# Decode attention with a gating MLP on one core: extra rows of w4 on five engines, values 512-wide on four column groups, y as one wide row

## The chip, the core and the metric

The kernel runs on one core of a Trainium2 chip. The metric is the device time of one execution in microseconds, from the first to the last instruction on that core as the harness takes it; a profile of one execution shows where it goes. In what follows PE is TensorE (the matrix engine), DVE is VectorE, ACT is ScalarE, POOL is GpSimd and SP is SyncE, which issues the loads. PSUM is the memory that matmuls write to.

## The reference

One token attends to the last 4096 positions of a cache of 32 heads, and the result is multiplied by a gate that a small MLP computes from the same token:

```python
x  = A_x                                  # 1 x 1 x 512, bf16
xn = layernorm(x)
q  = xn @ wq                              # 32 heads of 128
p  = softmax(q . k[last 4096] * 128**-0.5)
o  = p @ v[last 4096]                     # 32 heads of 128
s  = o.reshape(4096) @ wo                 # 4096 -> 512
h  = gelu(layernorm(xn) @ w1)             # S = 1: every one of its four shifted quarters becomes zero
x1 = xn + shifted(h) @ w2                 # the shifted h is zero
g  = silu(x1 + gelu(layernorm(x1) @ w3) @ w4)   # w3: 512 x 1376, w4: 1376 x 512
out = x + s * g
```

With one position the shifts leave only zeros, so the kernel never reads w1. Keys and values are 64 MB of the 78.84 MB that the kernel reads; wq and wo are 4 MB each, and the MLP's weights the rest.

## The kernel before

The heads are worked in eight groups of four (G = 4). In stage s the keys of group s are loaded and scored while the values of group s - 2 are used (LAG = 2). A tile of keys or values is 128 partitions by CP = 128 positions by 128 elements: 4 MB. All the large loads go out on SP's queue in program order; K tiles have three buffers, V tiles two.

The weights come first. The 1376 rows of w4 are ten blocks of 128 and 96 rows, and wq is read in two blocks of rows:

```python
w4_sb = wts.tile([P, 11, D], BF16, name="w4_sb")
load(w4_sb[:, 0:10, :], B_w4[0:10 * P, :].rearrange("(p c) n -> p c n", p=P))
load(w4_sb[0:96, 10, :], B_w4[10 * P:F, :])
...
load(wq_sb[:].rearrange("p c n -> p (c n)"), A_wq.rearrange("(a b c) n -> b a (c n)", a=2, c=KC))
```

The scores of a group are shared: VectorE multiplies and sums 64 to 80 of the 128 positions (`k_vector`, in four parts), and TensorE transposes the others, ScalarE copies them out of PSUM, and TensorE multiplies them with q (`k_turn`, `k_scores`). The values are multiplied in one of two forms. Groups 0 and 2 (`MOVED`) take the 16 columns of probabilities as the stationary operand and stream 512 elements of V; all 32 of these matmuls add into the same 16 rows of PSUM, and `v_add` then picks four 128-wide pieces out. The others take V as the stationary operand, in 128 narrow matmuls:

```python
def v_part(g, v, c0=0, c1=CP):
    s = st[g]
    if g in MOVED:
        s["ov"] = ps_o.tile([4 * G, 4, Dh], FP32, tag="oT", name="ov")
        for c in range(0, CP, 4):
            nc.tensor.matmul(s["ov"][:], lhsT=s["pT"][:, c:c + 4, :].rearrange("p i a -> p (i a)"),
                             rhs=v[:, c:c + 4, :], start=(c == 0), stop=(c == CP - 4))
        s["ov_sb"] = sm_pool.tile([4 * G, 4, Dh], FP32, tag="ov_sb", bufs=1, name="ov_sb")
        nc.scalar.copy(out=s["ov_sb"][:], in_=s["ov"][:])
        return
    if c0 == 0:
        s["oT"] = ps_o.tile([P, G], FP32, tag="oT", name="oT")
    for c in range(c0, c1):
        nc.tensor.matmul(s["oT"][:], lhsT=v[:, c, :], rhs=s["pT"][:, c, :], start=(c == 0),
                         stop=(c == CP - 1))
```

The output row y = o @ wo is added up in blocks of heads. Heads 0-15 are a wide row (16 matmuls of 1 x 512) in stage 6; heads 16-23 are 128-wide matmuls on four column groups (`y_block`). 320 rows of wo from head 24 on come by two loads over five DMA engines (`load_few`); the rest of wo comes as single rows of heads (`load_rows`):

```python
blocks = [(0, 16), (16, 8), (24, 8)]
...
def load_few():
    t = wo_blk[few_block]
    for c in range(2):
        r0 = few_h * P + c * FEW // 2
        load(t[32 * c:32 * c + 4 * NE],
             A_wo[r0:r0 + FEW // 2, :].rearrange("(b a t) n -> a b (t n)", b=4, a=NE))
```

The stages, with the parts of keys and softmax cut:

```python
if s < NG:
    k_open(s); k_vector(s, kn, 0); keys(0, 2)
    if s > 1:
        sm_den(s - 2); sm_rden(s - 2)
    if h - 1 in MOVED:                 # h = s - 2
        v_add(h - 1); v_out(h - 1)
    keys(2, 4); k_vector(s, kn, 1); ...
    keys(4, nb); k_scores(s, nb - 1); sm_own(s)
    if s > 0:
        sm_exp(s - 1)
    k_vector(s, kn, 2); ...; k_vector(s, kn, 3)
    if h >= 0:
        v_part(h, v)
    sm_max(s)
    if s == 6:
        y_wide(0, 0, 16)
    if h >= 0 and h not in MOVED:
        v_out(h)
elif s == NG:
    sm_den(NG - 2); sm_rden(NG - 2); sm_turn(NG - 1)
    ox_spread(1); sm_exp(NG - 1); ox_pick(1)
    y_block(1)
    rows_add(y_ps, one_f, y_row, False)
    v_part(h, v); v_out(h)
    ox_spread(few_block); sm_den(NG - 1); sm_rden(NG - 1)
    ox_pick(few_block); ox_few(few_block)
else:
    v_part(h, v, 0, cuts[1])           # cuts = (0, 64, 112, 128)
    y_block(few_block)
    for r in range(h_part, H - G):
        y_head(r)
    for c0, c1 in zip(cuts[1:], cuts[2:]):
        v_part(h, v, c0, c1)
    v_out(h)
    for r in range(H - G, H):
        y_head(r)
```

PE, DVE and ACT run these instructions in this order (`manual_schedule`).

Of the kernel before, what the change touches and what calls it, by code (L numbers as in the profile page):

```python
# [25 lines left out]
MOVED = (0, 2)  # L26
# [3 lines left out]
def kernel(  # L30
# [28 lines left out]
    assert F == 10 * P + 96  # L59
# [30 lines left out]
    w4_sb = wts.tile([P, 11, D], BF16, name="w4_sb")  # L90
    load(w4_sb[:, 0:10, :], B_w4[0:10 * P, :].rearrange("(p c) n -> p c n", p=P))
    load(w4_sb[0:96, 10, :], B_w4[10 * P:F, :])
    wq_sb = wts.tile([P, KC, HD], BF16, name="wq_sb")

    load(wq_sb[:].rearrange("p c n -> p (c n)"), A_wq.rearrange("(a b c) n -> b a (c n)", a=2, c=KC))
# [80 lines left out]

    x_f = small.tile([P, KC], FP32, name="x_f")
# [8 lines left out]
    perm = wts.tile([P, P // 2, 2], BF16, name="perm")  # L186
    nc.vector.tensor_copy(out=perm[:], in_=ident_bf[:].rearrange("k (a b) -> k b a", a=2))
# [24 lines left out]
    chunks = [(P, slice(r, 10 * P, 10)) for r in range(10)]  # L212
    chunks += [(96, slice(10 * P, F, 1))]
    a_ps = ps_misc.tile([P, 11], FP32, tag="misc", name="a_ps")
    for j, (m, cols) in enumerate(chunks):
        for c in range(KC):
            nc.tensor.matmul(a_ps[0:m, j:j + 1], lhsT=w3_sb[:, c, cols], rhs=z3_bf[:, c:c + 1],  # L217
                             start=(c == 0), stop=(c == KC - 1))
    a_bf = small.tile([P, 11], BF16, name="a_bf")
    nc.scalar.activation(out=a_bf[:, 0:10], in_=a_ps[:, 0:10], func=ACT.Gelu_apprx_tanh)  # L220
    nc.scalar.activation(out=a_bf[0:96, 10:11], in_=a_ps[0:96, 10:11], func=ACT.Gelu_apprx_tanh)
# [5 lines left out]
    for i, (m, _) in enumerate(chunks):  # L227
        nc.tensor.matmul(hr_ps[:], lhsT=a_bf[0:m, i:i + 1], rhs=w4_sb[0:m, i, :], start=False,  # L228
                         stop=(i == len(chunks) - 1))
# [31 lines left out]

    few = const.tile([P, 2, 32], BF16, name="few")
    nc.vector.memset(few[:], 0.0)
    for c in range(2):
        nc.vector.tensor_copy(
            out=few[:, c, 0:4 * NE].rearrange("p (a b) -> p a b", b=4),
            in_=ident_bf[:, 4 * NE * c:4 * NE * (c + 1)].rearrange("p (b a) -> p a b", b=4))


# [18 lines left out]
                            op0=ALU.add, op1=ALU.mult)  # L290

# [93 lines left out]
    blocks = [(0, 16), (16, 8), (24, 8)]  # L385
    few_block = 2
    few_h = blocks[few_block][0]
    FEW = 8 * 8 * NE
    h_part = few_h + FEW // P

    r_part = FEW % P
# [6 lines left out]
    def load_few():  # L398
        t = wo_blk[few_block]
        for c in range(2):  # L400
            r0 = few_h * P + c * FEW // 2
            load(t[32 * c:32 * c + 4 * NE],
                 A_wo[r0:r0 + FEW // 2, :].rearrange("(b a t) n -> a b (t n)", b=4, a=NE))

# [3 lines left out]
    def load_rows(h, n):  # L408
        if h == h_part:
            load(wo_rows[r_part:P, 0, :], A_wo[h * P + r_part:(h + 1) * P, :])  # L410
            h, n = h + 1, n - 1
        load(wo_rows[:, h - h_part:h - h_part + n, :],
             A_wo[h * P:(h + n) * P, :].rearrange("(h p) n -> p h n", p=P))
# [3 lines left out]
    def v_part(g, v, c0=0, c1=CP):  # L417
        s = st[g]
        if g in MOVED:
            s["ov"] = ps_o.tile([4 * G, 4, Dh], FP32, tag="oT", name="ov")  # L420
            for c in range(0, CP, 4):
                nc.tensor.matmul(s["ov"][:], lhsT=s["pT"][:, c:c + 4, :].rearrange("p i a -> p (i a)"),  # L422
                                 rhs=v[:, c:c + 4, :], start=(c == 0), stop=(c == CP - 4))
            s["ov_sb"] = sm_pool.tile([4 * G, 4, Dh], FP32, tag="ov_sb", bufs=1, name="ov_sb")
            nc.scalar.copy(out=s["ov_sb"][:], in_=s["ov"][:])  # L425
            return
        if c0 == 0:
            s["oT"] = ps_o.tile([P, G], FP32, tag="oT", name="oT")
        for c in range(c0, c1):
            nc.tensor.matmul(s["oT"][:], lhsT=v[:, c, :], rhs=s["pT"][:, c, :], start=(c == 0),  # L430
                             stop=(c == CP - 1))

    def v_add(g):
        s = st[g]
        s["oT"] = ps_misc.tile([P, G], FP32, tag="misc", name="oT")
        for j in range(4):
            nc.tensor.matmul(s["oT"][:], lhsT=s["ov_sb"][:, j, :], rhs=ident_f[0:4 * G, G * j:G * j + G],  # L437
                             start=(j == 0), stop=(j == 3))

    def v_out(g):  # L440
        h = G * g
        b = [i for i, (h0, _) in enumerate(blocks) if h >= h0][-1]
        if b not in o_blk:
            o_blk[b] = sm_pool.tile([P, blocks[b][1]], BF16, tag=f"o{b}", bufs=1, name="o")
            if b == few_block:
                nc.gpsimd.memset(o_blk[b][:], 0.0)
        c = h - blocks[b][0]
        if g >= NG - 2:
            nc.vector.tensor_tensor(out=o_blk[b][:, c:c + G], in0=st[g]["oT"][:], in1=st[g]["rden"][:],  # L449
                                    op=ALU.mult)  # L450
            return
        for k in range(G):
            nc.scalar.mul(o_blk[b][:, c + k:c + k + 1], st[g]["oT"][:, k:k + 1], st[g]["rden"][:, k:k + 1])  # L453
# [24 lines left out]
    def ox_few(i):  # L478
        of_ps = ps_misc.tile([64, 8], FP32, tag="misc", name="of_ps")
        nc.tensor.matmul(of_ps[:], lhsT=few[:].rearrange("p a b -> p (a b)"), rhs=ox_blk[i][:],  # L480
                         start=True, stop=True)
        of = sm_pool.tile([64, 8], BF16, tag="of", bufs=1, name="of")
        nc.vector.tensor_copy(out=of[:], in_=of_ps[:])
        ox_blk[i] = of


# [4 lines left out]
    def y_wide(i, t0, t1):  # L491
        n = blocks[i][1]
        if t0 == 0:
            yr[i] = ps_tr.tile([1, D], FP32, tag="pt", name="yr_ps")
        for t in range(t0, t1):
            nc.tensor.matmul(yr[i][:], lhsT=ox_blk[i][:, t:t + 1], rhs=wo_blk[i][:, t, :], start=(t == 0),  # L496
                             stop=(t == n - 1))
        if t1 == n:
            nc.scalar.copy(out=y_row[:], in_=yr[i][:])

    def y_block(i):
        for t in range(8):
            rows_add(y_ps, ox_blk[i][:, t:t + 1], wo_blk[i][:, t, :], False)

    def y_head(h):
        rows_add(y_ps, o_blk[few_block][:, h - few_h:h - few_h + 1], wo_row(h), h == H - 1)
# [7 lines left out]
    for s in range(NG + LAG):  # L514
# [3 lines left out]
        if s == LAG:  # L518
            wts_guard.__exit__(None, None, None)
            v_pool = ctx.enter_context(tc.tile_pool(name="v", bufs=V_BUFS))  # L520
            wo_blk[few_block] = v_pool.tile([64, 8, D], BF16, tag="wo_few", bufs=1, name="wo_few")
            nc.gpsimd.memset(wo_blk[few_block][:], 0.0)
            wo_rows = v_pool.tile([P, H - h_part, D], BF16, tag="wo_rows", bufs=1, name="wo_rows")
            nc.gpsimd.memset(wo_rows[0:r_part, 0, :], 0.0)
        if last:
            load_rows(h_part, 2)
            v = load_kv(v_pool, A_v_cache, h, cuts)
            for r, n in ((H - G, 2), (H - 2, 1), (H - 1, 1)):
                load_rows(r, n)
        elif h >= 0:  # L530
            v = load_kv(v_pool, A_v_cache, h)
# [4 lines left out]
        if h == 5:  # L536
            load_wo(1)
            load_few()

        if s < NG:  # L540
# [14 lines left out]
            if h - 1 in MOVED:  # L555
                v_add(h - 1)
                v_out(h - 1)
# [18 lines left out]
            if s == 6:  # L576
                y_wide(0, 0, 16)
            if h >= 0 and h not in MOVED:
                v_out(h)
        elif s == NG:  # L580

            sm_den(NG - 2)
            sm_rden(NG - 2)
            sm_turn(NG - 1)
            ox_spread(1)
            sm_exp(NG - 1)
            ox_pick(1)
            y_block(1)
            rows_add(y_ps, one_f, y_row, False)
            v_part(h, v)  # L590
            v_out(h)
            ox_spread(few_block)
            sm_den(NG - 1)
            sm_rden(NG - 1)
            ox_pick(few_block)
            ox_few(few_block)
        else:
            v_part(h, v, 0, cuts[1])
            y_block(few_block)
            for r in range(h_part, H - G):  # L600
                y_head(r)
            for c0, c1 in zip(cuts[1:], cuts[2:]):
                v_part(h, v, c0, c1)
            v_out(h)
            for r in range(H - G, H):
                y_head(r)
# [36 lines left out]
```

## Time and profile before

| what | value |
|---|---|
| time, median of 3 runs | 194.84 us (194.61 to 195.24) |
| span of the profiled execution | 193.2 us |
| busy PE, DVE, ACT, POOL | 132.6, 143.8, 87.1, 6.4 us |
| read from HBM | 78.84 MB, 408 GB/s over the span |
| DMA packets | 4725, of them 1466 under 2 KB |
| mean granted clock of PE | 0.702 |

The profile is one execution on this core. Its page gives the busy time of each engine, then the span in 40 slices of 4.83 us with a digit for the busy tenths, then the DMA queues, then the groups of instructions by line: busy us and mean ns of one, then the idle time before them and what ended it. A timeline line gives start, length, engine, source line, and output<-inputs. "issue" is a wait that the profile doesn't explain. The granted clock is TensorE's own, as a share of full speed. Matmuls overlap, so the mean duration of one is longer than what it costs in a row.

### The profile page before, as it was taken

To read this page: it belongs to the slowest core of one execution; us is meant where nothing else is said; L and a number is where in the kernel's file an instruction comes from. 1 tells how busy PE (TensorE), PEld (TensorE's weight loads), DVE (VectorE), ACT (ScalarE), POOL (GpSimd) and SP (SyncE) were. 2 spreads that over 40 slices of the span, in tenths; PEclk is the share of its full clock that TensorE was granted. 3 is DMA by queue.
4 is the path that set the end of the run, shared out by engine and by line. 5 is a ranking of instruction groups with operands and counts; after the bars stand their busy time and mean duration, and the time that the engine had idled before them with its cause. 6 is when DMAs were issued, how large, how long until landed. Compare 5 with 4: busy or idle time off the path is not lost.

```text
span 193.2 us, 4769 instructions
## 1 busy us (share of the span) xinstructions
PE 132.6 (69%) x2123; PEld 102.3 (53%) x2123; DVE 143.8 (74%) x162; ACT 87.1 (45%) x195; POOL 6.4 (3%) x14
## 2 busy tenths in 40 slices
PE   0549763977736579798898938840878879845792
PEld 0444463866625433486884428740768257733771
DVE  0560208999999999999999999990899999931201
ACT  2003002888896360468568044731574077813000
POOL 2110008000000000000000000000000000000000
PEclk9999955588755557978559995855576696755555
DMA  6999999999999999999999999999999999999980
GB/s 205 417 472 427 397 427 453 421 427 424 434 431 434 434 433 421 434 427 434 424 431 434 431 434 407 461 431 434 431 427 426 427 424 407 458 417 377 416 326 8
DMA packets 4725, 79.13 MB, mean 410 GB/s; under 512 B 666, under 2 KB 1466, under 8 KB 1722
## 3 DMA queue, kind: packets, MB, share of 16 engines
q1 hardware_dynamic: 4554, 78.84, 96.0%
q8 instruction: 16, 0.26, 0.5%
q10 hardware_dynamic: 152, 0.00, 0.0%
q14 instruction: 3, 0.02, 0.0%
HBM read 78.84 MB, written 0.00 MB: 408 GB/s over the span
## 4 chain that ended last, share of the span: by engine, by line
DVE 50%; DMA 24%; PE 16%; issue 5%; ACT 3%; POOL 1%; SPq 0%; ACTq 0%; POOLq 0%
DVE S L310 29%; DVE prod L308 16%; DMA kv<-in_A_k_cache_dram 14%; DMA kv<-in_A_v_cache_dram 8%; PE oT L430 3%; PE yr_ps L496 3%; ACT kt L326 2%; DMA x_bf<-in_A_x_dram 2%; PE qT_ps L244 2%; PE hr_ps L228 2%; PE a_ps L217 1%; PE pt L324 1%; PE hr_ps L225 1%; PE sT L332 1%; DVE S L346 1%
## 5 line engine op out<-in xcount | busy, mean ns | idle before, releaser
L310 DVE TENSOR_REDUCE S<-prod 128x20 f32<-128x2560 bf16 (+2 forms) x32 | 82.2, 2570 | 1.1
L326 ACT COPY kt<-pt 128x1024 bf16<-128x1024 bf16 (+1 forms) x56 | 54.5, 1007 | 20.9 <-PE pt L324 20.3
L324 PE MATMUL pt<-ident_bf,kv 128*128 128x128 bf16 x444 | 47.1, 276 | 7.1 <-DMA kv<-in_A_k_cache_dram 7.1
L308 DVE TENSOR_TENSOR prod<-kv,q_bc 128x2560 bf16<-128x2560 bf16 (+2 forms) x32 | 43.5, 1360 | 7.6 <-DMA kv<-in_A_k_cache_dram 4.9
L324 PEld LDWEIGHTS <-kv 128*128 128x128 bf16 x444 | 38.0, 127 | 9.2 <-DMA kv<-in_A_k_cache_dram 7.9
L332 PE MATMUL sT<-qT_bf,kt 128*128 128x4 bf16 x444 | 20.6, 168 | 16.9 <-ACT kt L326 16.3
L332 PEld LDWEIGHTS <-kt 128*128 128x128 bf16 x444 | 17.1, 103 | 24.5 <-ACT kt L326 24.1
L430 PE MATMUL oT<-pT,kv 128*128 128x4 bf16 x768 | 21.8, 166 | 7.6 <-issue 5.5
L430 PEld LDWEIGHTS <-kv 128*128 128x128 bf16 x768 | 21.1, 103 | 9.6 <-issue 5.7
L422 PE MATMUL ov<-kv,pT 128*16 128x512 bf16 x64 | 16.6, 425 | 0.0
L370 ACT ACTIVATE pT<-S,mb 128x128 bf16<-128x128 f32 x32 | 13.9, 570 | 0.3
L453 ACT ACTIVATE o<-oT,rden 128x1 bf16<-128x1 f32 x24 | 4.3, 261 | 15.5 <-PE oT L430 9.0
L422 PEld LDWEIGHTS <-pT 128*16 128x16 bf16 x64 | 6.1, 98 | 9.5 <-issue 3.5
L449 DVE TENSOR_TENSOR o<-oT,rden 128x4 bf16<-128x4 f32 x2 | 0.3, 162 | 12.4 <-PE oT L430 12.4
L341 ACT ACTIVATE own<-sT,par 128x48 f32<-128x48 f32 (+2 forms) x32 | 7.6, 361 | 3.6 <-PE sT L332 3.1
L370 ACT ACTIVATION_READ_ACCUMULATOR pT<-S,mb 128x1 f32 x32 | 8.2, 255 | 0.0
L231 DVE COPY hr<-hr_ps 1x512 f32<-1x512 f32 x1 | 0.7, 679 | 8.3 <-PE hr_ps L228 8.3
L425 ACT COPY ov_sb<-ov 16x512 f32<-16x512 f32 x2 | 1.1, 575 | 12.1 <-PE ov L422 12.1
L437 PE MATMUL oT<-ident_f,ov_sb 16*128 16x4 f32 x16 | 2.9, 301 | 4.1 <-DVE rden L381 4.1
L496 PE MATMUL yr_ps<-wo,ox 128*1 128x512 bf16 x16 | 4.9, 476 | 1.2 <-DVE ox L474 1.2
L220 ACT ACTIVATE a_bf<-a_ps 128x10 bf16<-128x10 f32 x1 | 0.2, 179 | 12.1 <-PE a_ps L217 12.1
L354 PE MATMUL mt_ps<-ident_f,m 128*1 128x128 f32 x8 | 2.8, 354 | 3.3 <-DVE rden L381 3.3
(117 smaller groups left out, 92.0 us busy)
## 6 DMA issues: line engine op xcount, KB each, us to landing
kv<-in_A_k_cache_dram SPq DMA_DIRECT2D x7, 4096.0 KB, 29.4
kv<-in_A_v_cache_dram SPq DMA_DIRECT2D x7, 4096.0 KB, 33.8
wq_sb<-in_A_wq_dram SPq DMA_DIRECT2D x1, 4096.0 KB, 18.4
kv<-in_A_k_cache_dram SPq DMA_DIRECT2D x2, 2048.0 KB, 22.6
wo<-in_A_wo_dram SPq DMA_DIRECT2D x1, 2048.0 KB
kv<-in_A_v_cache_dram SPq DMA_DIRECT2D x1, 2048.0 KB, 11.9
kv<-in_A_v_cache_dram SPq DMA_DIRECT2D x1, 1536.0 KB, 15.0
w_sb<-in_B_w_dram SPq DMA_DIRECT2D x1, 1376.0 KB
```

Source lines behind the costliest of these rows:

```text
L228: nc.tensor.matmul(hr_ps[:], lhsT=a_bf[0:m, i:i + 1], rhs=w4_sb[0:m, i, :], start=False, stop=(i == len(chunks) - 1))
L308: nc.vector.tensor_tensor(out=prod[:, 0:m, :], in0=kn[:, rows, :], in1=q_bc[:, g:g + 1, :].to_broadcast([P, m, Dh]), op=ALU.mult)
L310: nc.vector.tensor_reduce(out=st[g]["S"][:, rows], in_=prod[:, 0:m, :], axis=AX.X, op=ALU.add)
L324: nc.tensor.transpose(pt[:, c - c0, :], kn[:, c, :], ident_bf[:])
L326: nc.scalar.copy(out=kts[b][:, 0:c1 - c0, :], in_=pt[:, 0:c1 - c0, :])
L332: nc.tensor.matmul(st[g]["sT"][:, c - nd(g), :], lhsT=kt[:, c - c0, :], rhs=qT_bf[:, G * g:G * g + G], start=True, stop=True)
L341: nc.scalar.mul(s["own"][:, 0:m, a], s["sT"][:, 0:m, a], par[:, a:a + 1])
L370: nc.scalar.activation(out=s["pT"][:, :, a], in_=s["S"][:], func=ACT.Exp, scale=scale, bias=mb[:, a:a + 1], accum_out=s["sum"][:, a:a + 1])
L422: nc.tensor.matmul(s["ov"][:], lhsT=s["pT"][:, c:c + 4, :].rearrange("p i a -> p (i a)"), rhs=v[:, c:c + 4, :], start=(c == 0), stop=(c == ...
L430: nc.tensor.matmul(s["oT"][:], lhsT=v[:, c, :], rhs=s["pT"][:, c, :], start=(c == 0), stop=(c == CP - 1))
L453: nc.scalar.mul(o_blk[b][:, c + k:c + k + 1], st[g]["oT"][:, k:k + 1], st[g]["rden"][:, k:k + 1])
L496: nc.tensor.matmul(yr[i][:], lhsT=ox_blk[i][:, t:t + 1], rhs=wo_blk[i][:, t, :], start=(t == 0), stop=(t == n - 1))
```

## The change

It moves where the uneven load of five DMA engines falls, and puts values and y into forms with fewer and wider matmuls. TensorE's program goes from 4,120 rows to 3,026.

- 320 rows of w4 are loaded over five engines, as 320 rows of wo were; w4 is now 8 blocks of 128, 32 rows and these 320. Their activations are brought onto the right partitions by a small product (`few`), and the 1 x 512 row is added up from 17 chunks instead of 11. wq comes in four blocks of rows, with the permutation of x to match.
- All groups take the wide form of values, and successive matmuls go to four groups of 16 rows at partitions 0, 32, 64 and 96 of one PSUM tile, which a zero product opens. `v_add` adds the four groups through a folded identity. In the last group only the first 64 positions are wide; the rest is narrow and adds to the same sum.
- y of heads 0-27 is one row of 1 x 512: 16 + 8 matmuls in stage 8 and 4 in stage 9. Only heads 28-31 stay as rows of heads. The wo block of heads 24-27 is a plain load of 512 KB.

```diff
-MOVED = (0, 2)
+MOVED = (0, 1, 2, 3, 4, 5, 6, 7)
...
-    load(w4_sb[:, 0:10, :], B_w4[0:10 * P, :].rearrange("(p c) n -> p c n", p=P))
-    load(w4_sb[0:96, 10, :], B_w4[10 * P:F, :])
+    load(w4_sb[:, 0:8, :], B_w4[0:8 * P, :].rearrange("(p c) n -> p c n", p=P))
+    load(w4_sb[0:32, 8, :], B_w4[F - 32:F, :])
+    w4_few = wts.tile([64, 8, D], BF16, name="w4_few")
+    nc.gpsimd.memset(w4_few[:], 0.0)
+    for c in range(2):
+        f0 = 8 * P + 32 * NE * c
+        load(w4_few[32 * c:32 * c + 4 * NE],
+             B_w4[f0:f0 + 32 * NE, :].rearrange("(b a t) n -> a b (t n)", b=4, a=NE))
-    load(..., A_wq.rearrange("(a b c) n -> b a (c n)", a=2, c=KC))
+    load(..., A_wq.rearrange("(a b c) n -> b a (c n)", a=4, c=KC))
...
-    chunks = [(P, slice(r, 10 * P, 10)) for r in range(10)]
-    chunks += [(96, slice(10 * P, F, 1))]
+    chunks = [P] * 8 + [32] + [8 * NE] * 8
...
+    af_ps = ps_misc.tile([64, 8], FP32, tag="misc", name="af_ps")
+    nc.tensor.matmul(af_ps[:], lhsT=few[0:8 * NE].rearrange("p a b -> p (a b)"), rhs=a_bf[0:8 * NE, 9:17], ...)
...
-    blocks = [(0, 16), (16, 8), (24, 8)]
+    blocks = [(0, 16), (16, 8), (24, 4), (H - G, G)]
...
     def v_part(g, v, c0=0, c1=CP):
-        if g in MOVED:
-            s["ov"] = ps_o.tile([4 * G, 4, Dh], FP32, tag="oT", name="ov")
-            ... (one group of rows)
+        if c0 == 0 and g in MOVED:
+            n = CP if g < NG - 1 else c1
+            s["ov"] = ps_o.tile([P, 4, Dh], FP32, tag="oT", name="ov")
+            nc.tensor.matmul(s["ov"][:], lhsT=zero_bf[:], rhs=zero_bf[:]..., start=True, stop=False, ...)
+            for i in range(n // 4):
+                c, r = 4 * i, 32 * (i % 4)
+                nc.tensor.matmul(s["ov"][r:r + 4 * G], lhsT=s["pT"][:, c:c + 4, :]...,
+                                 rhs=v[:, c:c + 4, :], start=False, stop=(i >= n // 4 - 4), ...)
...
-            nc.tensor.matmul(s["oT"][:], lhsT=s["ov_sb"][:, j, :], rhs=ident_f[0:4 * G, G * j:G * j + G],
+            nc.tensor.matmul(s["oT"][:], lhsT=s["ov_sb"][:, j, :], rhs=fold[:, G * j:G * j + G],
...
-            load_rows(h_part, 2)
             v = load_kv(v_pool, A_v_cache, h, cuts)
...
-            load_few()
+            load_wo(2)
...
-            if h - 1 in MOVED:
+            if h > 0:
                 v_add(h - 1)
                 v_out(h - 1)
...
-            if s == 6:
-                y_wide(0, 0, 16)
-            if h >= 0 and h not in MOVED:
-                v_out(h)
         elif s == NG:
             sm_den(NG - 2); sm_rden(NG - 2); sm_turn(NG - 1)
+            v_add(h - 1)
+            v_out(h - 1)
             ox_spread(1); sm_exp(NG - 1); ox_pick(1)
-            y_block(1)
-            rows_add(y_ps, one_f, y_row, False)
+            y_wide(0, True, False)
+            y_wide(1, False, False)
             v_part(h, v)
+            v_add(h)
             v_out(h)
-            ox_spread(few_block); ...; ox_few(few_block)
+            ox_spread(2); ...; ox_pick(2)
         else:
             v_part(h, v, 0, cuts[1])
-            y_block(few_block)
-            for r in range(h_part, H - G):
-                y_head(r)
+            y_wide(2, False, True)
+            v_add(h)
             for c0, c1 in zip(cuts[1:], cuts[2:]):
                 v_part(h, v, c0, c1)
+            rows_add(y_ps, one_f, y_row, False)
             v_out(h)
```

## The prediction

> **What bounds the kernel now.** I read the page's slices first, then the table of DMA queues, then the tail in the windows view and the timeline, because a stream that is never idle leaves only its ends to change.
>
> ```profile
> PEclk9999955588755557978559995855576696755555
> DMA  6999999999999999999999999999999999999980
> ...
> q1 hardware_dynamic: 4554, 78.84, 96.0%
> q8 instruction: 16, 0.26, 0.5%
> ```
>
> The DMA row is at nine tenths or more from the second slice to the 38th. Queue 1 moves 78.84 MB and fills 96.0% of 16 engines' span. So 185.5 of 193.2 us is transfer, and the rest is about 1.7 us before the first packet and the last 4 us. No load changes its bytes, so the middle can give little. The tail is what can move, in the windows view (columns: window and length, then busy us and count of PE, PEld, DVE, ACT, POOL, then the granted clock, the DMA share, GB/s):
>
> ```profile
> 166.00:171.40 5.40, 3.85 (x132) 3.75 (x131) 4.14 (x5) 2.64 (x14) 0.00 (x0) 0.56 1.04 444
> 171.40:178.00 6.60, 3.08 (x47) 1.81 (x48) 1.23 (x6) 2.58 (x13) 0.00 (x0) 0.50 0.97 382
> 178.00:183.30 5.30, 4.34 (x132) 4.03 (x132) 1.09 (x6) 0.00 (x0) 0.00 (x0) 0.50 1.00 419
> 183.30:187.00 3.70, 3.41 (x105) 2.62 (x106) 0.12 (x1) 0.00 (x0) 0.00 (x0) 0.50 0.91 365
> ```
>
> TensorE runs at half clock here, yet has room: between 171.4 and 178.0 it is busy 3.08 of 6.60 us. Its steps in the timeline (start, length, engine, line):
>
> ```profile
> 166.07 3.43 PE L430 MATMUL oT<-pT,kv 128*128 128x4 bf16 x124
> ...
> 174.68 1.02 PE L150 MATMUL y_ps<-wo,ox 128*1 128x128 bf16 x32 [0.62 <-DVE ox L474]
> ...
> 177.96 3.57 PE L430 MATMUL oT<-pT,kv 128*128 128x4 bf16 x128 [1.73 <-DMA kv<-in_A_v_cache_dram]
> ...
> 183.34 1.87 PE L430 MATMUL oT<-pT,kv 128*128 128x4 bf16 x64
> ...
> 186.98 1.87 PE L430 MATMUL oT<-pT,kv 128*128 128x4 bf16 x64 [0.19 <-DMA kv<-in_A_v_cache_dram]
> 188.88 0.16 DVE L449 TENSOR_TENSOR o<-oT,rden 128x4 bf16<-128x4 f32 x1 [5.46 <-PE oT L430]
> ```
>
> Three times (177.96, 183.34, 186.98) PE is ready and V is not: the loads set the end, and PE's slack before the last is only about 0.2 us (0.5 for the weights). The last 16 y matmuls end at 189.76 and the output follows. The group rows give the prices:
>
> ```profile
> L430 PE MATMUL oT<-pT,kv 128*128 128x4 bf16 x768 | 21.8, 166 | 7.6 <-issue 5.5
> ...
> L422 PE MATMUL ov<-kv,pT 128*16 128x512 bf16 x64 | 16.6, 425 | 0.0
> ...
> L496 PE MATMUL yr_ps<-wo,ox 128*1 128x512 bf16 x16 | 4.9, 476 | 1.2 <-DVE ox L474 1.2
> ```
>
> A narrow V matmul (L430) costs 3.57/128 = 28 ns in a row, whatever the mean of 166 says (they overlap). A 512-wide one costs 0.427 us at half clock and 0.215 at full; I read both spacings from the 16 of L496, where the clock rose after 2.7 us.
>
> **What the Trainium skill says.** "TensorE: Matmul & The Clock Gate", Part 1: PE's clock is halved when idle, and about 3.4 us of activity releases it. The trace agrees: L496 went from 0.427 to 0.215 us within its burst, and from 166.7 us to the end the clock is 0.5. The same page, Part 3, says matmuls on different column groups overlap, measured 2.38x for three groups and 3.07x for four row groups. Here the 32 of L150 on four groups took 1.02 us, 32 ns for 128 columns at half clock, where one group's 512-wide takes 107 per 128: 3.3x. "DMA: Bandwidth & Descriptors", "Why a DMA increments its semaphore by 16 and not by 1": the number of engines divides both slowest dimensions, and the lowest-numbered are taken; 5 and 20 give five engines. No row of the trace names engines; the packets of the few-row loads are 8 KB, four to an engine, which fits. "Runtime: NRT & Kernel Launch", Instruction fetch mechanics: 16 KiB blocks of 256 instructions. PE has 4,120 instructions before, 16.1 blocks, and q8 shows 16 packets.
>
> **Part by part.**
>
> Loads. 320 rows of wo over five engines become 320 rows of w4 over five: equal imbalance, 64 KB more on each of five, earlier. 1 KB packets drop from 800 to 544. One lasts 46 ns against 38 per KB in the large ones, so 256 x 8 ns / 16 = 0.13 us off each engine. PE instructions drop to 3,026, 12 blocks; following packets engine by engine, I find an engine falls back about 1.5 us per fetch, so four fewer are 0.4 us of the mean; the last engine may gain nothing. Sum: -0.1 to -0.9 us on the last landing. Four blocks of wq: the 32 KB packets stay 32 KB, and that load already ran at 433 GB/s: 0.
>
> Start. a_ps goes from 44 to 68 matmuls: 24 x 63 ns (2.79/44) = 1.5 us. hr_ps goes from 15 to 21: 6 x 0.215 to 0.427 = 1.3 to 2.6. The small product and copy add 0.5. The q product waits behind this chain (its PSUM buffer is released by bv at 22.97), so the first prod moves from 29.75 to about 33. The loads then have K1 and K2 queued to about 50 us, and DVE has 4.9 us of idle later (L308 waiting for K, once), so this is absorbed: 0. The 3.5 us clear of the few-row tile moves onto Pool's start; identity is needed at 7.4 us and is ready near 5: 0.
>
> Middle. 128 narrow matmuls (3.6 us) become 33 wide ones: 32 x 0.215 / 3.07 + 0.2 = 2.4 us at full clock, 4.9 at half. Groups 0 and 2 fall from 6.9 or more. PE is not the bound there: 0.
>
> Tail. This is where I expect the cost, since wide y (16 + 8) now stands in front of the V product of group 6. Step by step:
> - Keys of group 7: the addition of group 4's four columns now stands behind rden (158.53) and takes 0.75 us (full clock) to 1.86 (half, both in the trace). Keys resume near 160 instead of 157.8; ScalarE saves 0.9 before; six copies of 1.02 follow. V of group 5 starts near 167.5 instead of 166.07. It takes 2.4 to 4.9 us without the old stall of 1.55, and ends near 170.5.
> - Then the max transposition, addition (0.75 to 1.86), four o of 0.72 in all, spread, ox: about 5 us. Wide y starts near 175.5.
> - 24 wide: 7 at 0.427 until the clock rises, 17 at 0.215: 6.7 us, to 182.2. Before, the 40 narrow in its place took 1.6 us and V6 began at 177.96.
> - V6: 2.4, to 184.6. Copy 0.6, addition 0.75, o, spread and ox product 0.85: to 186.8.
> - First half of V7: 17 wide, 1.3, to 188.1. Wide y of block 2: 0.9. Addition 0.75. To 189.7.
> - The 64 narrow of the rest 1.9, the y row 0.4, the heads 0.66: 192.7, against 189.76. So +2.9 us.
>
> Once PE sets the end, the landing gain no longer counts: 194.84 + 2.9 = about 197.8.
>
> **The rivals.** (1) The stream still sets the end. For it: 96.0% transfer, and all V waits before are on DMA. It needs wide y near 174 and the full clock, 24 x 0.215 = 5.2 us, to 179.2; then every later step is 3 us earlier and the end is within 0.3 us of before, less up to 0.9: 194.0 to 195.1. (2) The clock stays at half: wide y 10.2 us, V6 4.9, the first half of V7 2.5, the two additions 1.1 each more. That is +8, about 203. Against it: L496 recovered in 2.7 us, and 24 in a row are denser. (3) The late start eats more than DVE's 4.9 us and delays K6: perhaps +2. Against it: DVE still waits for K6, and loads keep 10 us or more of queue. (4) Five engines lagging from the start delay every landing by up to 2.5 us: but all loads share it and the sum per engine is unchanged, so only intermediate waits grow: +0 to 1.
>
> **Range and chances.** The main sum gives +2.9; its largest uncertain terms are the start of wide y (2 us each way) and the clock (up to 3 below, 5 above). Rival 1 sets the low edge, 194.6; a partly halved clock the high one, 200.6. A gain of 2% would be 3.9 us, to below 190.9: the bytes at the rate of before do not allow it, 0.03. Slower by 2% is above 198.7: 0.34. Within: 0.63.
>
> **What would show it.** Right: between 175 and 190 PE has no V wait above 0.5 us, wide y sits before V6, V6 starts past 180, and the gap from the landing of V7's last part to the final y matmul grows from 2.8 us (186.9 to 189.76). Queue 8 shows 12 packets. Wrong: PE still waits for V at the last part (rival 1), the clock of the tail reads 0.5 throughout (rival 2), the DMA row shows a slice below 9 in the middle (rival 3). My prediction falls if wide y starts before 173, or if four column groups give less than 2x.

## The result, and the profile after

The changed kernel takes 201.09 us, median of 7 runs (199.64 to 201.25), against 195.24 us (194.61 to 196.14) for the kernel before on the same chip: a ratio of 1.027, 95% interval 1.0232 to 1.0308. The prediction was 197.8 us with a range up to 200.6: the direction came out, and so did the mechanism (PE and no longer the loads sets the end); the size of one step did not.

The profile of the changed kernel is that of its quickest run, 199.64 us. First the lines of its page that answer to the four shown of before, with the line that sums the chain of waits by engine:

```profile
PEclk9999965795555556757696585567576856687995
DMA  6999999999999999999999999999999999999800
...
q1 hardware_dynamic: 4410, 78.84, 93.8%
q8 instruction: 12, 0.20, 0.4%
...
DVE 50%; PE 29%; DMA 13%; issue 4%; ACT 3%; POOL 0%; POOLq 0%; ACTq 0%; SPq 0%
```

The stream is as full as before, but it ends earlier in the picture: the last slice of loads is the 38th of 40 slices that are now 4.95 us long. In absolute time the last packet of 1 KB lands at 188.9 us, against 189.1 before. So nothing was lost in the loads; what got longer is what comes after them. In the chain PE's share went from 16% to 29% and that of DMA from 24% to 13%. The windows of the tail (window and length; busy us and count of PE, PEld, DVE, ACT, POOL; granted clock, DMA share, GB/s), cut at the steps of the prediction:

```profile
...
177.00:183.80 6.80, 6.80 (x25) 2.20 (x24) 0.49 (x2) 1.55 (x8) 0.00 (x0) 0.76 0.97 405
...
188.70:191.80 3.10, 3.09 (x31) 1.68 (x31) 0.35 (x2) 1.16 (x2) 0.00 (x0) 1.00 0.01 2
```

In the first of these rows PE is busy for all of 6.80 us, the wide y. In the last, 3.09 of 3.10 us of PE's work is still to do with the DMA share at 0.01. Before, PE had room until the last 3 us and the stream was at 0.91 up to 187. The steps in the timeline (start, length, engine, line):

```profile
158.87 1.87 PE L446 MATMUL oT<-fold,ov_sb 128*128 128x4 f32 x8 [1.26 <-DVE rden L402]
...
169.58 3.26 PE L432 MATMUL ov<-kv,pT 128*16 128x512 bf16 x32
...
174.37 1.03 PE L446 MATMUL oT<-fold,ov_sb 128*128 128x4 f32 x8 [0.47 <-DVE mx L377]
...
176.98 6.92 PE L493 MATMUL yr_ps<-wo,ox 128*1 128x512 bf16 x24
...
184.15 1.90 PE L432 MATMUL ov<-kv,pT 128*16 128x512 bf16 x32
...
193.79 0.57 PE L156 MATMUL y_ps<-wo_rows,o 128*1 128x128 bf16 x16
```

None of them waits for V any more: the three waits of before on a DMA are gone. V of group 6 starts at 184.15 instead of 177.96, and the last matmul ends at 194.36 instead of 189.76: +4.6 us. The first line is the one to remember: the addition of group 4, which the change puts among the keys of group 7, takes 1.87 us, after a wait of 1.26. The group rows show how little the wide forms cost in PE time as such:

```profile
L432 PE MATMUL ov<-kv,pT 128*16 128x512 bf16 x240 | 23.0, 551 | 0.0
...
L446 PE MATMUL oT<-fold,ov_sb 128*128 128x4 f32 x64 | 11.7, 305 | 15.6 <-DVE rden L402 14.5
```

The additions take 11.7 us of PE, half as much as all 240 wide V matmuls, and their idle time of 15.6 us is mostly for `rden`, the reciprocal sums of the softmax that VectorE computes. (An addition is four float32 products in the program; the profile shows each as two, so eight to an addition.)

### The profile page after: what moved, and what is told of

It is laid out like the page before. It is cut to its first block, busy times and chain, and to the rows that moved or that the text cites. A ratio compares the mean times of both kernels' runs of the same rounds, so it can differ in the third digit from the quotient of the medians.

```text
span 197.8 us, 3773 instructions
## 1 busy us (share of the span) xinstructions
PE 137.2 (69%) x1621; PEld 96.8 (49%) x1621; DVE 145.3 (73%) x167; ACT 91.7 (46%) x202; POOL 5.9 (3%) x12
## 4 chain that ended last, share of the span: by engine, by line
DVE 50%; PE 29%; DMA 13%; issue 4%; ACT 3%; POOL 0%; POOLq 0%; ACTq 0%; SPq 0%
DVE S L331 28%; DVE prod L329 15%; DMA kv<-in_A_k_cache_dram 11%; PE oT L446 4%; PE yr_ps L493 4%; PE pt L345 3%; PE ov L432 3%; PE hr_ps L255 3%; PE a_ps L236 2%; DMA x_bf<-in_A_x_dram 2%; PE qT_ps L271 2%; ACT kt L347 1%; PE sT L353 1%; PE hr_ps L250 1%; PE oT L439 1%
## 5 line engine op out<-in xcount | busy, mean ns | idle before, releaser
L345 PE MATMUL pt<-ident_bf,kv 128*128 128x128 bf16 x444 | 48.7, 282 | 5.4 <-DMA kv<-in_A_k_cache_dram 5.4
L345 PEld LDWEIGHTS <-kv 128*128 128x128 bf16 x444 | 39.7, 130 | 9.8 <-DMA kv<-in_A_k_cache_dram 7.0
L432 PE MATMUL ov<-kv,pT 128*16 128x512 bf16 x240 | 23.0, 551 | 0.0
L446 PE MATMUL oT<-fold,ov_sb 128*128 128x4 f32 x64 | 11.7, 305 | 15.6 <-DVE rden L402 14.5
L446 PEld LDWEIGHTS oT<-fold,ov_sb 128*128 128x128 f32 x64 | 11.0, 259 | 17.2 <-DVE rden L402 14.9
L436 ACT COPY ov_sb<-ov 128x512 f32<-128x512 f32 x8 | 4.7, 586 | 21.0 <-PE ov L432 21.0
L432 PEld LDWEIGHTS <-pT 128*16 128x16 bf16 x240 | 6.8, 115 | 13.2 <-issue 12.0
L456 DVE TENSOR_TENSOR o<-oT,rden 128x4 bf16<-128x4 f32 x2 | 0.3, 162 | 14.5 <-PE oT L446 10.2
L493 PE MATMUL yr_ps<-wo,ox 128*1 128x512 bf16 x28 | 7.9, 446 | 0.0
L384 PE MATMUL mb_ps<-md,par_t 5*128 5x4 f32 x16 | 4.0, 320 | 2.8 <-DVE md L379 2.0
## 6 DMA issues: line engine op xcount, KB each, us to landing
kv<-in_A_v_cache_dram SPq DMA_DIRECT2D x1, 2048.0 KB, 10.2
```

The lines of the kernel that those rows point to most:

```text
L345: nc.tensor.transpose(pt[:, c - c0, :], kn[:, c, :], ident_bf[:])
L432: nc.tensor.matmul(s["ov"][r:r + 4 * G], lhsT=s["pT"][:, c:c + 4, :].rearrange("p i a -> p (i a)"), rhs=v[:, c:c + 4, :], start=False, sto ...
L446: nc.tensor.matmul(s["oT"][:], lhsT=s["ov_sb"][:, j, :], rhs=fold[:, G * j:G * j + G], start=(j == 0), stop=(j == 3 and g < NG - 1))
L493: nc.tensor.matmul(yr["ps"][:], lhsT=ox_blk[i][:, t:t + 1], rhs=wo_blk[i][:, t, :], start=(first and t == 0), stop=(stop and t == blocks[i ...
```

## The experiments

My theory after the result: PE's tail sets the end, and the extra time is in it; which of its parts, and at which clock, was open. The rival was that the loads of the change (late start, five uneven engines) cost it. All kernels are edits of the changed kernel. Medians and ranges are of all runs; the ratios, to the kernel before on the same chip, leave out runs more than 1.5% above the fastest of their kernel, which matters for e1, e2, e10 and e11.

| kernel | us, median (range) | ratio (95% interval) |
|---|---|---|
| e1 loads as before | 201.76 (199.43 to 202.93) | 1.0309 (1.0238 to 1.0381) |
| e2 y of heads 0-15 in stage 6 | 198.15 (194.95 to 201.23) | 1.0042 (1.0021 to 1.0064) |
| e3 values as before | 196.48 (196.10 to 196.96) | 1.0079 (1.0051 to 1.0108) |
| e4 y as before | 199.17 (198.30 to 200.21) | 1.0218 (1.0167 to 1.0269) |
| e5 values of groups 4-7 narrow | 195.83 (195.07 to 196.35) | 1.0022 (1.0003 to 1.0040) |
| e6 e5 and y as before | 195.04 (194.93 to 196.44) | 0.9991 (0.9975 to 1.0007) |
| e7 new loads alone | 195.00 (194.87 to 195.88) | 0.9982 (0.9965 to 0.9999) |
| e8 addition later in the stage | 205.29 (204.11 to 206.33) | 1.0508 (1.0457 to 1.0558) |
| e9 changed kernel again | 201.86 (201.09 to 203.18) | 1.0347 (1.0295 to 1.0398) |
| e10 products of zeros in PE's gaps | 198.91 (196.42 to 202.45) | 1.0101 (1.0049 to 1.0153) |
| e11 e2 with these products | 195.56 (194.97 to 200.01) | 1.0011 (0.9978 to 1.0043) |
| e12 values of group 4 narrow | 197.52 (196.78 to 197.66) | 1.0105 (1.0077 to 1.0133) |

### Loads: e1 and e7

e1 takes back the loads of w4 and wq with their chunks, and keeps the rest:

```diff
-    load(w4_sb[:, 0:8, :], ...); load(w4_sb[0:32, 8, :], ...); (w4_few over five engines)
+    load(w4_sb[:, 0:10, :], ...); load(w4_sb[0:96, 10, :], ...)
-    load(..., A_wq.rearrange("(a b c) n -> b a (c n)", a=4, c=KC))
+    load(..., A_wq.rearrange("(a b c) n -> b a (c n)", a=2, c=KC))
```

> The changed kernel with w4, the 11 chunks of the MLP and wq in two blocks as before; no load goes over five engines any more. Tail theory (PE's work in front of the last values sets the end; the later start of the first product, 33.4 instead of 29.8 us, is absorbed before stage 7): the start comes back by about 3.5 us and the end by less than 0.7, so 200.4 to 201.1 us. Load theory (five late engines and the longer MLP chain cost the time): 198 us or less.

Measured: 201.76 us. The first `prod` (VectorE's first product of keys) is back at 29.75, and nothing is gained: the late start and the five engines are not the cause. e7 does the opposite. It keeps the loads of the change and takes back values and y:

```diff
-MOVED = (0, 1, 2, 3, 4, 5, 6, 7)
+MOVED = (0, 2)          # with v_part, v_add and v_out of before
-            y_wide(0, True, False); y_wide(1, False, False)
+            y_block(1); rows_add(y_ps, one_f, y_row, False)   # y_wide(0, True, True) in stage 6
-            y_wide(2, False, True)
+            y_block(2)
```

> The loads of the change alone: w4 on five engines, wq in four blocks, 4 KB packets for the wo rows of heads 24-27; values and y in the form of before. Tail theory: 194.3 to 195.3 us, no difference from before, although the first product starts 3.5 us later. Load theory: 196 to 198.

Measured: 195.00 us, ratio 0.9982: at best a gain of 0.2%, for the interval ends at 0.9999. The first `prod` comes at 32.18 us, 2.4 us later than before, and this is absorbed: the first `prod` of group 7 is at 155.07, against 155.08 before. V waits for its loads again:

```profile
178.25 3.57 PE L436 MATMUL oT<-pT,kv 128*128 128x4 bf16 x128 [2.65 <-DMA kv<-in_A_v_cache_dram]
183.14 1.31 PE L436 MATMUL oT<-pT,kv 128*128 128x4 bf16 x43 [0.45 <-DMA kv<-in_A_v_cache_dram]
186.83 1.87 PE L436 MATMUL oT<-pT,kv 128*128 128x4 bf16 x64 [0.32 <-DMA kv<-in_A_v_cache_dram]
```

### Values or y: e3, e4, e5, e6

e3 takes back the values alone, e4 the form of y alone:

```diff
 e3
-MOVED = (0, 1, 2, 3, 4, 5, 6, 7)
+MOVED = (0, 2)          # with v_part, v_add and v_out of before
 e4
-            y_wide(0, True, False); y_wide(1, False, False)
+            y_block(1); rows_add(y_ps, one_f, y_row, False)   # y_wide(0, True, True) in stage 6
-            y_wide(2, False, True)
+            y_block(2)
```

> The changed kernel with values as before: narrow in all groups but 0 and 2, those two on one group of rows. Tail theory: the stall of stage 7's keys behind rden and the additions of groups 5, 6 and 7 go (about 1.9 + 1.0 + 1.7 us with their copies), wide y stays in the tail: 2 to 4 us back, 197 to 199 us. Values theory: nearly all comes back, 195.5 to 196.5. Load theory: 201.

> The changed kernel with y as before in form: heads 0-15 wide in stage 6 and copied out there, heads 16-27 in narrow matmuls on four column groups (32 in stage 8, 16 in stage 9). Tail theory: V6 starts near 179, the end comes back by 4 to 5 us, 196 to 197 us. Values theory: 1 us back or less, 200. Load theory: 201.

Measured: 196.48 and 199.17 us. Less the kernel before on the same chip (194.89), that is +1.6 and +4.3 us, where the changed kernel has +5.9 on its own chip: taking back the values gives about 4.3, taking back y about 1.6. I had taken the wide y for the larger part; e4 says no. In e4 the 32 narrow y matmuls took only 1.02 us, but the products of group 6 that follow took 3.59 us where the changed kernel has 1.90, and the later addition 1.87 instead of 1.05: what y gave back was partly taken by a slower clock.

e5 makes the values narrow in groups 4 to 7 only, with y wide; e6 is e5 with y as in e4:

```diff
-MOVED = (0, 1, 2, 3, 4, 5, 6, 7)
+MOVED = (0, 1, 2, 3)    # other groups: narrow matmuls, no addition, o at the end of the stage
```

> The changed kernel with the values of groups 4 to 7 narrow; groups 0 to 3 stay 512-wide on four column groups, y stays one wide row. Tail theory (only what stands in stages 7 to 9 counts): as with all values undone, 196.1 to 197.0 us. Middle theory (the additions behind rden slow every stage): 198 us or more.

> The same, and y in the form of before as well (heads 0-15 in stage 6, 16-27 narrow on four column groups). What is left of the change: the loads, and wide values in groups 0 to 3. Tail theory: PE waits for V again and the last load sets the end: 194.2 to 195.2 us, a ratio of 0.997 to 1.001. If the five engines or the longer start cost something of their own: 196 or more.

Measured: 195.83 and 195.04 us. So the wide values of groups 0 to 3 cost nothing that shows (e6 against e7), and the wide y costs about 0.8 us (e5 against e6) even though in e5 its 24 matmuls take 7.24 us, from 173.09 on. What costs is the wide form of the last groups.

### The addition among the keys: e12 and e8

e12 takes the wide form from group 4 alone, whose addition stands among the keys of group 7:

```diff
-MOVED = (0, 1, 2, 3, 4, 5, 6, 7)
+MOVED = (0, 1, 2, 3, 5, 6, 7)
```

> Only the values of group 4 go back to narrow matmuls, so that no addition stands among the keys of group 7; all else is as changed. My theory: V of group 5 starts 1.0 to 2.5 us earlier, near 167, this passes to the end, and the median is 198.8 to 200.1. Rival (V of group 5 starts when ScalarE and VectorE let it, the addition was hidden): V of group 5 starts within 0.5 us of 169.3 and the median stays at 200.5 to 201.3.

Measured: 197.52 us, below what I gave it, and 4.3 us below the changed kernel on the same chip (e9), 3.5 between the two profiled runs. One group of eight brings about what taking back all values brings. The timeline of e12:

```profile
157.96 1.01 PE L345 MATMUL pt<-ident_bf,kv 128*128 128x128 bf16 x8
...
166.93 1.90 PE L432 MATMUL ov<-kv,pT 128*16 128x512 bf16 x32
...
171.27 1.84 PE L449 MATMUL oT<-fold,ov_sb 128*128 128x4 f32 x8 [0.46 <-DVE mx L377]
...
174.90 6.91 PE L496 MATMUL yr_ps<-wo,ox 128*1 128x512 bf16 x24
```

The keys go on at 157.96, as before the change (157.88), V of group 5 starts at 166.93, and the wide y at 174.90. The lines of the changed kernel in its second profile (e9, 201.09 us, a typical run) stand against these:

> The changed kernel once more, unaltered, for a second profile. Clock theory: the profiled run of 199.64 us had the full clock from 187 us on; in a run at the typical 201.1 us some of the same instructions take the half-clock times, that is the 32 wide V matmuls of group 6 about 3.6 us instead of 1.90 or an addition 1.85 instead of 1.05, and these differences add up to the 1.5 us. Rival: the later run has the same durations and a later start of the wide y (about 178.5), from the keys or the softmax.

```profile
158.91 1.87 PE L446 MATMUL oT<-fold,ov_sb 128*128 128x4 f32 x8 [1.00 <-DVE rden L402]
160.64 1.01 PE L345 MATMUL pt<-ident_bf,kv 128*128 128x128 bf16 x8
...
169.63 3.59 PE L432 MATMUL ov<-kv,pT 128*16 128x512 bf16 x32
...
174.85 1.84 PE L446 MATMUL oT<-fold,ov_sb 128*128 128x4 f32 x8 [0.46 <-DVE mx L377]
...
178.48 6.81 PE L493 MATMUL yr_ps<-wo,ox 128*1 128x512 bf16 x24
...
185.54 1.90 PE L432 MATMUL ov<-kv,pT 128*16 128x512 bf16 x32
```

Keys resume 2.7 us later than in e12 (160.64 against 157.96), V of group 5 starts 2.7 us later, and takes 3.59 instead of 1.90 us. The wide y starts 3.6 us later; the rest of the difference goes into waits for ScalarE and VectorE that e12 has after V of group 5. The slower V is a part of the delay: in both runs the granted clock is full from 164.4, but in e9 it drops at 167.8, before V of group 5 has begun, and in e12 at 171.2, after it has ended. Of the 2.7 us, 1.00 is the wait for `rden` and the rest the addition at half clock. No run computes `rden` earlier, so the two are not separated.

The delay passes through ScalarE, as its timeline in e9 shows:

```profile
160.82 0.72 ACT L460 ACTIVATE o<-oT,rden 128x1 bf16<-128x1 f32 x4 [2.85 <-PE oT L446]
161.69 2.08 ACT L347 COPY kt<-pt 128x1024 bf16<-128x1024 bf16 x2 [0.15 <-PE pt L345]
```

ScalarE stands still for 2.85 us until the addition is done, works 0.72 us at `o`, and only then copies the third batch of keys, at 161.69, 3.2 us later than before the change. The copies that follow take about a microsecond each, so little is won back: ScalarE's next step, `own`, starts at 168.68 against 165.87. The profile of before has this copy in the first of the next two lines. The second, from two stages earlier, was there as a warning: the one addition of that stage, among the keys of group 5, kept ScalarE idle for 4.98 us.

```profile
158.52 1.93 ACT L326 COPY kt<-pt 128x1024 bf16<-128x1024 bf16 x2 [0.23 <-PE pt L324]
...
118.46 0.72 ACT L453 ACTIVATE o<-oT,rden 128x1 bf16<-128x1 f32 x4 [4.98 <-PE oT L437]
```

The second profile also tests how the typical 201 us differ from the profiled 199.64. The wide y starts 1.50 us later (178.48 against 176.98), but not because anything ahead of V of group 5 is later: that starts at 169.63 against 169.58. In between, 0.33 us is V of group 5 (3.59 against 3.26) and 0.81 the addition of group 5 (1.84 against 1.03), that is, a clock that rises later, as the clock expectation had it for an addition; the rest is in the small steps between them. V of group 6 takes 1.90 us in both.

Why the clock rises later can partly be read from the two traces. In both, a stretch at one clock lasts 3.41 us or a multiple of it, so the clock can change only at certain points, and these fall differently in the two runs. In the three rows below (the first from the profile of the changed kernel, the others from e9; window and length, busy us and count of PE, granted clock, DMA share, GB/s), each window reaches from one such point to the next:

```profile
169.96:173.37 3.41, 3.40 (x33) 0.50 1.03 437
...
167.84:171.25 3.41, 2.98 (x27) 0.50 1.02 437
171.25:174.67 3.42, 2.86 (x23) 0.50 0.95 398
```

In the first, V of group 5 fills the window, and the next one is at full clock. In e9 a point falls into the middle of V, neither window is full, and the clock rises only at 181.5, 3.0 us into the wide y. That a filled window raises the clock fits these two runs, but isn't shown as a rule: in e3, 3.29 us of transpositions and small products in one window, and 3.33 us of narrow V matmuls in another, raised nothing.

e8 moves the addition, with `o`, in stages 2 to 7 behind the fourth batch of keys and the transposition of the maxima, to let keys go first:

```diff
             keys(0, 2); sm_den(s - 2); sm_rden(s - 2)
-            v_add(h - 1); v_out(h - 1)
             keys(2, 4); k_vector(s, kn, 1); sm_turn(s - 1)
+            v_add(h - 1); v_out(h - 1)
             keys(4, nb)
```

> The changed kernel with one order changed: in stages 2 to 7 the addition of the four groups and its output come after the keys' third and fourth batch and the max transposition, so those no longer stand behind rden. Tail theory with the stall of stage 7 as the mis-sized term: V5 starts 1.5 us earlier (168 instead of 169.3), wide y near 175.5, the end 1.0 to 1.8 us earlier, 199.3 to 200.1 us. If the stall is filled by ScalarE's copies anyway: no change, 201.

Measured: 205.29 us; the idea was wrong. The addition now comes behind a product of VectorE (`mx`), `o` comes behind the addition, and ScalarE's copies of the last batches come behind `o`. ScalarE in stage 7 of e8:

```profile
166.43 0.72 ACT L460 ACTIVATE o<-oT,rden 128x1 bf16<-128x1 f32 x4 [6.83 <-PE oT L446]
```

V of group 5 starts at 173.26, 3.6 us later than in e9, and the end is 3.7 us later (span 203.0 against 199.3). So this delay of V of group 5 passes to the end one to one. In e12 a start 2.7 us earlier makes the last matmul end 3.5 us earlier (192.28 against 195.78), the other 0.8 being the faster V less the waits behind it.

### The clock of the tail: e2, e10, e11

e2 moves the first 16 wide y matmuls from stage 8 to the end of stage 6:

```diff
             sm_max(s)
+            if s == 6:
+                y_wide(0, True, False)
...
-            y_wide(0, True, False)
             y_wide(1, False, False)
```

> The changed kernel with the 16 wide y matmuls of heads 0-15 put back into stage 6; their sum stays open in PSUM until stage 9. Tail theory: 16 of the 24 wide matmuls leave the stretch ahead of V6, which then starts near 180.5 instead of 183.8; the end comes back by 2.5 to 3.5 us, 197.5 to 198.6 us, less if the clock then stays at half. Load theory: no change, 201. Values theory (the additions and copies of the wide values cost the time, not y): at most 1 us back.

Measured: 198.15 us over 20 runs, but from 194.95 to 201.23, roughly in step with the granted clock: the five runs at 0.727 to 0.729 and the one at 0.734 took 194.95 to 195.60, the three at 0.703 took 198.33 to 198.66, the three at 0.664 took 201.22 or 201.23 (but 195.80 came at 0.694, and 199.75 at 0.713). The kernel before shows nothing of the sort: with clocks from 0.663 to 0.717, 12 of its 15 runs beside e9 are within 194.50 and 195.65. In these runs a tail that PE bounds was exposed to the clock, and one that waits for loads was not. The mean clock of a whole run is a poor gauge of this, though; over the four runs of e1 the longer ones have the higher mean.

e10 tests it by a direct change. Seven 512-wide products of zeros, read by nobody, are put into PE's gaps in stage 8:

```diff
             sm_turn(NG - 1)
+            filler(3)
             v_add(h - 1)
+            filler(4)
             v_out(h - 1)
```

> Seven 512-wide products of zeros, whose result nobody reads, stand where TensorE waits in stage 8: three ahead of the addition of group 5, four behind it, ahead of the wide y. Clock theory: TensorE's clock is up when the 24 wide y begin, they take 5.2 to 5.6 us instead of 6.85, V of group 6 takes 1.9 to 2.3, and the time falls by 1.0 to 2.0 us, to 199.3 to 200.3 in the median. Rival (the place of the work on TensorE alone counts, not the clock): the fillers only add to the queue, the time is 201 to 202.

Measured: 198.91 us, 2.9 below e9 on the same chip. These are four runs, from 196.42 to 202.45 where e9 has 201.09 to 203.18, so the size is rough. The timeline of the profiled run (197.98 us) shows what the fillers did:

```profile
170.01 3.16 PE L432 MATMUL ov<-kv,pT 128*16 128x512 bf16 x32
...
173.87 0.81 PE L504 MATMUL fill<-zero_bf 128*128 128x512 bf16 x3
174.51 1.01 PE L446 MATMUL oT<-fold,ov_sb 128*128 128x4 f32 x8
175.38 1.02 PE L504 MATMUL fill<-zero_bf 128*128 128x512 bf16 x4
...
177.08 5.34 PE L493 MATMUL yr_ps<-wo,ox 128*1 128x512 bf16 x24
```

The wide y takes 5.34 us instead of 6.81, because the clock is up when it begins (24 x 0.215 would be 5.2), and it begins 1.4 us earlier than in e9: 1.47 + 1.40 = 2.9 of the 3.1 us between the two profiled runs. Only the first part is the fillers' work. The clock rose at 172.6, during V of group 5, and the first filler came at 173.87; the earlier begin is the same luck as in the first profile of the changed kernel, where V took 3.26 us, the addition 1.03, and the wide y began at 176.98 (here 177.08). There the clock fell again at 176.8, and the wide y took 6.92 us; with the fillers it stayed up. The like comparison gives 1.6 us, nearly all of the 1.7 between these two runs (199.64 and 197.98). So the rival, that the fillers only add to the queue, falls. But two of the four runs took 199.85 and 202.45 us: the fillers held a clock that had risen in the profiled run, and not in every run.

e11 puts both together:

> The kernel with y of heads 0-15 in stage 6, with the same seven products of zeros in the waits of stage 8. Without them its times ran from 194.95 to 201.23 us, in step with the granted clock. Clock theory: the tail is at full clock in every run, the median falls from 198.15 to 195.0 to 196.3, and the spread to below 2 us. Rival (the clock of the tail follows something earlier than its own gaps): median 197.5 to 198.7 and the same spread of 6 us.

Measured: 195.56 us; ten of the twelve runs are between 194.97 and 196.70, two at clocks of 0.682 and 0.683 near 200, so the median came as the clock expectation had it and the spread of below 2 us did not. In the profiled one the last V waits for its load again:

```profile
186.87 1.79 PE L439 MATMUL oT<-pT,kv 128*128 128x4 bf16 x64 [0.69 <-DMA kv<-in_A_v_cache_dram]
```

With the wide forms all in place, the stream sets the end once more, at about the time of the kernel before: none of these runs shows a gain from them.

## Why the prediction was wrong

- Loads, "-0.1 to -0.9 us on the last landing": right in size. The last 1 KB packet is 0.2 us earlier, queue 8 shows 12 packets, and e7 (still 16 packets there) has 0.9982. But "about 1.5 us per fetch" was too high: by the page of before, the 16 packets of queue 8 took 0.5% of 16 engines' span, about 1 us each, so four fewer are about 0.25 us of the mean.
- Start, absorbed: right. The first `prod` came at 33.36 (about 33 was predicted), that of group 7 at 155.19 (155.08 before). Rivals 3 and 4 fall with this and with e1.
- Middle, 0: right (e5 and e6: wide values in groups 0 to 3 cost nothing).
- Tail, the shape: right. PE has no V wait, the wide y stands ahead of V of group 6, and the gap from the landing to the end grew. Rival 1 fell; it is what e7 and e11 show.
- Tail, the size: wrong, in one step, "V of group 5 starts near 167.5 instead of 166.07 ... and ends near 170.5". In the typical run (e9) it starts at 169.63 and ends at 173.2. I had the keys resume near 160; they did so at 160.64 (0.6 late). From there I gave 7.5 us to the start of V, with 0.9 us of ScalarE's time saved, and it was 9.0 (1.5 late). The keys alone, up to the product `mb` ahead of V, took 7.9 us as before the change (157.88 to 165.76, 160.64 to 168.57): ScalarE saved nothing, because it sat idle for the addition and had `o` (0.72 us) in the middle of the keys instead of ahead of them. `mb` and the product of zeros that opens V's sum then took 1.06 us at half clock, where `mb` alone had taken 0.31. V of group 5 was 3.59 us instead of about 3.0 (0.6 late), and the steps to the wide y 5.3 instead of 5 (0.3). So the wide y starts at 178.48, 3.0 us after the predicted 175.5. From there on the terms hold: y 6.81 (6.7 predicted), V of group 6 1.90 (2.4), and the last matmul ends at 195.8, 3.1 after the predicted 192.7. Nearly the whole miss of 3.3 us (201.1 against 197.8) is this start of the wide y. That the rest agrees is partly luck: the additions of groups 6 and 7 were put at 0.75 us each and took 1.06 and 1.05, V of group 6 was put 0.5 us too long, and the wide y takes anything from 5.34 us (e10) to 7.24 (e5), depending on when the clock rises.
- The clock: rival 2, "wide y 10.2 us, V6 4.9", did not come: these took 6.81 and 1.90. Its sum was also wrong: over the main sum its terms are 3.5 + 2.5 + 1.2 + 2.2 = 9.4 us, which makes about 207 and not 203. And I looked for the half clock in the wrong place. It costs ahead of the wide y, in the two additions (1.87 and 1.84 us) and V of group 5 (3.59), and I took for granted that the sparse stretch before the wide y would be neutral. e10 shows that it isn't: the clock that was lost there cost 1.6 us in the first part of y.

What stays open: what it takes to raise the clock, and how much of the loss it makes in a given run. The runs show that its points of change fall differently from run to run, and that products in PE's gaps kept it up once it had risen.

## What to carry to other kernels

Before moving work to a cheaper form, look at where its follow-up stands in the in-order queues: here an addition of eight small matmuls among the keys of the last group held ScalarE's copies, and doing without this one of eight additions took back most of the loss. When a change takes slack from an engine that waited for loads, price that engine's tail at its low clock too, and expect the runs to spread, as in e2. And a step of a prediction that gives time back ("ScalarE saves") needs the same proof as one that costs.

## What the hardware showed unexpectedly

- On four column groups a 512-wide matmul took 59 ns at full clock (1.90 us for 32), 3.6 times quicker than the 215 ns of one group, and 112 ns at half clock (3.59 us). I had worked with 3.07.
- The narrow V matmuls hardly gained from the clock: 128 took 3.40 us in e3 at a granted clock of 0.94 and 3.57 before at 0.50; the additions in float32, four columns each, did (1.03 to 1.06 against 1.84 to 1.87 us).
- Seven products that nobody reads, on the engine that sets the end, made the 24 wide y matmuls behind them 1.6 us shorter (5.34 against 6.92 us); the medians of four runs each were 198.91 and 201.86.
- In the profiles of the changed kernel and of e9 every stretch at one granted clock lasts 3.41 us or a multiple of it.
